# Decay tables in one 128-partition transfer, a plan that models instruction blocks, and the first tile's states in two parts

## The chip, the cores and the metric

The kernel runs on one core of one Trainium2 chip, one launch. The metric is device time in microseconds (us): 421.51, the median of three runs (421.35 to 424.3). Engines are named as in the profile: PE (matrix products; PEld its weight loads), DVE, ACT, POOL, and SP, whose queue issues all the DMAs.

## The reference, cut to what matters

Three layers in a row, on 4 sequences of 768 tokens with 256 channels:

```python
# 1: linear attention with decay, 8 heads, state 16 x 32 a head, in chunks
L = exp(cum[i] - cum[j]) * causal            # cum: running sum of log a
y = ((C @ B.T) * L) @ x + (C @ state) * exp(cum)
state = exp(cum[last]) * state + B.T @ (x * exp(cum[last] - cum))
# 2: channel mix; the row before each token is mixed in (mu_k, mu_r)
k = maximum(xk @ w_k, 0) ;  v = (k * k) @ w_v
x = sigmoid(xr @ w_r) * v
# 3: maxout
out = maximum(maximum(x @ w1, x @ w2), x @ w3) @ w_out
```

The weights come as 64-bit floats. Each product of layers 2 and 3 is made of three: both sides are split into a high and a low 32-bit part, and high x high, high x low and low x high are added.

## The kernel before, in words

The tokens are cut into 6 tiles of 4 x 128 = 512 columns. A tile t goes through `attention(t)` (layer 1, chunks of 64 tokens), `gate` (w_r), `ffn` (w_k in `s2(f)`, w_v in `s3(f)`, f = 0 to 7, L977 to L992), `combine`, `maxout(t)` (L1028, L1030) and `final` (w_out, L1068), and the tiles are interleaved: layer 3 of tile t - 1 runs beside layer 1 of tile t + 1.

The steps of `attention(t)` on PE: `spread` (the decay matrix of tiles 0 and 1: L680 for tile 0; L695 to L703 for tile 1, in two halves, into the banks pb), `gather` (L749: the state that each chunk adds), `cb` (L826: C times B), `carried` (L851: what the state before gives), `yt` (L861: the sums over values). Then `masked` (L756 on ACT, L758 on DVE) keeps the wanted blocks of what gather made, `state(c)` (L764, L766) decays the state by a column of the tile `ec` and adds, L815 makes `ce` from `ec`, and L896 copies y from PSUM into `xb`, from which `mix` (L928 to L931) makes the inputs of `gate` and `ffn`. From tile 2 on the decay matrix is not made by `spread`: it is loaded from a table in DRAM (L<-crd) and finished on DVE and ACT. `sums()` (L583, L594, L587, L588, L596) makes these tables and `ccol`; `ec` (decays to every token) is loaded from the table `ced`.

Weights: `load_split` loads one block (h, wd, wol and others are staging tiles), ACT takes the magnitude (L613), four DVE instructions build the 32-bit float (L614, L616, L618, L620), and L397 on ACT and L405 on DVE (or POOL) make the two parts. The staging tiles are reused: a block's DMA can be issued only when DVE has read the block before it out of its tile (L620).

The order of the work is not written out. Every step is an `op` with a cost for each engine it can run on, its buffers and a bias; the class `Plan` runs a list scheduler over them, 60 rounds, and issues the best order it has found. Each engine then executes its own list strictly in that order. The parts of the plan that the change touches:

- `BLOCK` and `CALM`: before, an op on PE marked as a burst (many small products) is put behind another one when more than 136 such products would fall into 4 us.
- `EARLY`: PE starts with 100 narrow products on zeros (L1131).
- `filler`: where the plan sees PE idle before the first `gate`, it issues products that nobody reads (L1129).
- `plan.wait_for`: the ops of which the earliest ends the stretch with fillers.

A program's instructions are themselves fetched by DMA, in blocks (the queues "instruction" in part 3 of the profile). The code in which the changed steps stand follows.

Of the kernel before, what the change touches and what calls it, by code (L numbers as in the profile page):

```python
# [75 lines left out]
class Plan:  # L76
# [16 lines left out]
    CALM = 4000.0  # L93
    BLOCK = 136
    HEAVY = (2100.0, 16000.0, 1300.0)
    WARM = (3400.0, 430.0, 215.0, 100.0, 600.0)
    EARLY = 100
# [39 lines left out]
    def forward(self, key, spare):  # L137
# [10 lines left out]
        runs = []  # L148
        done = 0

        def finish(i, e, now, fin):
            start[i], where[i], end[i] = now, e, fin
            for s in succ[i]:
                missing[s] -= 1
                ready_at[s] = max(ready_at[s], fin + self.lat(e, self.on[s]))
                if missing[s] == 0:
                    heapq.heappush(pending, (ready_at[s], s, ""))
                    heapq.heappush(events, ready_at[s])

        while done < n:  # L160
# [16 lines left out]
            for e in self.ENGINES:  # L177
# [5 lines left out]
                if e == "PE" and ops[q[0][1]][7] and ops[q[0][1]][7] + sum(  # L183
                        k for at, k in runs if at > now - self.CALM) > self.BLOCK:
# [34 lines left out]
                else:  # L219
                    if e == "PE" and now < self.COLD:  # L220
                        cost = cost * 1.35
                    if e == "PE" and ops[i][7]:
                        runs.append((now + cost, ops[i][7]))
# [104 lines left out]
def kernel(  # L328
# [242 lines left out]
    def initial():  # L571
        pe0 = boot.bufs[0]
# [170 lines left out]
    def gather(t, p):  # L743
        for b in range(NB):
            for q in range(NQ4):
                g = (q * NB + b) * 2
                for c in range(2):
# [21 lines left out]
    def attention(t):  # L769
# [11 lines left out]
        if first:  # L781
            inputs(0, FIRST)
        else:
            b_ec.writers, b_ec.readers = [dma(
                260, ec[32 * q:32 * q + 32].rearrange("p b c i -> p (b c i)"),
                ced[t * NG + q * NU:t * NG + (q + 1) * NU].rearrange("(r b) x -> r (b x)", r=2)[:, None, :].to_broadcast([NR, N, NU * HP]),
                r=[b_ced[t // (NT // 2)]], after=base, first=early) for q in range(NQ4)], []
# [12 lines left out]
        plan.bias += BIAS[5] * first  # L800
        if t < 2:
            op("PE", 64 * 10.8 + SWITCH, lambda: gather(t, U), r=[b_bd, b_xt[t]], w=U, burst=64)

        for c in range(2 if more else 1):
# [3 lines left out]
            else:  # L808
                masked(um[:, c], uv, [U[c]], [b_um[c]])
        if not first:  # L810
            state(0)
# [52 lines left out]
        if more:  # L864
            bias, plan.bias = plan.bias, 0.0
            inputs(t + 1, [EARLY1 * first] * 2)
# [16 lines left out]
        plan.bias -= BIAS[3] * first  # L883
        if more:
# [51 lines left out]
    def gate(half, t):  # L936
# [3 lines left out]
        for c2 in range(KC):  # L940
# [11 lines left out]
            plan.wait_for.append(begun['gate'])  # L952
# [5 lines left out]
    def ffn(half, t):  # L958
# [4 lines left out]
        def s2(f):  # L963
# [3 lines left out]
            def go():  # L967
                terms = []
                for c in range(KC):
                    terms.extend(three([w[:, c, fs] for w in wk_t], [v[:, cols] for v in xkt[c]]))  # L970
                mm3(p.ap[:, :n], terms)

            begun[f] = pe(6 * n * 0.4441, go, flat(b_xkt, hv) + [b_wk[c][f // 4] for c in range(KC)], [p])
# [211 lines left out]
```

## Time and profile before

| | |
|---|---|
| median of three runs | 421.51 us |
| profiled execution | 420.81 us |
| its span (first to last instruction) | 418.7 us |
| PE busy | 402.2 us, 96% |
| DVE busy | 260.4 us, 62% |
| ACT busy | 214.4 us, 51% |
| PE idle, by the table of waits | 12.9 us in 8 waits |

The span is cut into 40 slices in part 2 of the page; a digit is a tenth of the slice. PE stands at 9 in all but five slices (1, 3, 8, 23 and 39, counted from 0). DVE stands at 9 in many of the slices up to the fifteenth and falls to 4 or 5 afterwards. So the first third is shared by two engines near their limit, and after it PE alone is full.

### The profile page before, as it was taken

To read this page: it belongs to the slowest core of one execution; us is meant where nothing else is said; L and a number is where in the kernel's file an instruction comes from. 1 tells how busy PE (TensorE), PEld (TensorE's weight loads), DVE (VectorE), ACT (ScalarE), POOL (GpSimd) and SP (SyncE) were. 2 spreads that over 40 slices of the span, in tenths; PEclk is the share of its full clock that TensorE was granted. 3 is DMA by queue.
4 is the path that set the end of the run, shared out by engine and by line. 5 is a ranking of instruction groups with operands and counts; after the bars stand their busy time and mean duration, and the time that the engine had idled before them with its cause. 6 is when DMAs were issued, how large, how long until landed. Compare 5 with 4: busy or idle time off the path is not lost.

```text
span 418.7 us, 8689 instructions
## 1 busy us (share of the span) xinstructions
PE 402.2 (96%) x3681; PEld 320.1 (76%) x3681; DVE 260.4 (62%) x420; ACT 214.4 (51%) x374; POOL 54.2 (13%) x59
## 2 busy tenths in 40 slices
PE   9695999989999999999999989999999999999996
PEld 5464778768887888878888867888887888888885
DVE  5697889799997895465564466374465215440532
ACT  5575876786477672154762144763244752222221
POOL 4100000000200510142140033140022200010010
PEclk9789799999999999999999999999999999999999
DMA  7954636940126600022400000500000000001001
GB/s 251 392 160 138 201 88 204 266 125 2 53 92 178 159 26 0 17 89 77 125 25 2 10 19 2 125 2 26 0 3 2 25 25 2 0 0 44 8 2 50
DMA packets 12879, 31.55 MB, mean 75 GB/s; under 512 B 1768, under 2 KB 4136, under 8 KB 12072
## 3 DMA queue, kind: packets, MB, share of 16 engines
q1 hardware_dynamic: 12840, 30.99, 23.8%
q8 instruction: 29, 0.48, 0.5%
q14 instruction: 10, 0.08, 0.1%
HBM read 27.64 MB, written 3.34 MB: 74 GB/s over the span
## 4 chain that ended last, share of the span: by engine, by line
PE 73%; DVE 13%; DMA 7%; issue 3%; ACT 2%; SPq 1%; DVEq 0%; ACTq 0%
PE pa L665 40%; PE pa L992 13%; PE pa L1068 10%; PE pa L949 2%; DMA h<-in_w_v_dram 2%; DMA L<-crd 2%; PE pb L1068 2%; DVE tmp L1030 2%; DMA h<-in_w_r_dram 2%; PE pb L826 2%; DVE k2l L405 2%; SPq L410 1%; DMA ec<-ced 1%; PE pb L851 1%; PE pb L861 1%
## 5 line engine op out<-in xcount | busy, mean ns | idle before, releaser
L1030 DVE TENSOR_TENSOR tmp<-tmp,pa 128x512 f32<-128x512 f32 x72 | 48.9, 683 | 52.9 <-PE pa L665 52.1
L397 ACT ACTIVATE hr<-tmp 128x512 fp32r<-128x512 f32 x36 | 22.7, 632 | 75.2 <-DVE tmp L1030 74.8
L405 DVE TENSOR_TENSOR k2l<-tmp,k2h 128x512 fp32r<-128x512 f32 x52 | 37.3, 730 | 37.6 <-ACT tmp L980 30.8
L992 PE MATMUL pa<-k2l,wvh 128*128 128x512 f32 x96 | 38.0, 396 | 1.5 <-DVE k2l L405 1.5
L992 PE MATMUL pa<-k2h,wvh 128*128 128x512 f32 x96 | 38.1, 397 | 0.0
L992 PE MATMUL pa<-k2h,wvl 128*128 128x512 f32 x96 | 38.0, 396 | 0.0
L1068 PE MATMUL pa<-hr,worh 128*128 128x512 f32 x120 | 37.5, 393 | 0.0
L977 ACT ACTIVATE tmp<-pa 128x512 f32<-128x512 f32 x48 | 28.3, 591 | 10.9 <-PE pa L665 9.7
L978 ACT ACTIVATE k2h<-tmp 128x512 fp32r<-128x512 f32 x48 | 30.3, 631 | 3.0 <-PE pa L992 1.8
L1028 ACT ACTIVATE tmp<-pa 128x512 f32<-128x512 f32 x36 | 21.4, 594 | 18.3 <-PE pa L665 17.3
L405 DVE TENSOR_TENSOR hr<-tmp,hr 128x512 fp32r<-128x512 f32 x28 | 20.8, 745 | 13.4 <-ACT hr L397 13.3
L1068 PEld LDWEIGHTS pa<-hr,worh 128*128 128x128 f32 x120 | 22.2, 188 | 5.4 <-ACT th L954 0.6
L405 POOL TENSOR_TENSOR hr<-tmp,hr 128x512 fp32r<-128x512 f32 x8 | 10.8, 1354 | 108.0 <-ACT hr L397 108.0
L980 ACT ACTIVATE tmp<-tmp 128x512 f32<-128x512 f32 x37 | 23.2, 630 | 0.7
L1068 PE MATMUL pa<-hr,worl 128*128 128x512 f32 x60 | 23.3, 389 | 0.0
L992 PEld LDWEIGHTS pa<-k2l,wvh 128*128 128x128 f32 x96 | 18.0, 188 | 6.6 <-DVE k2l L405 2.6
L992 PEld LDWEIGHTS pa<-k2h,wvh 128*128 128x128 f32 x96 | 18.0, 188 | 4.3
L992 PEld LDWEIGHTS pa<-k2h,wvl 128*128 128x128 f32 x96 | 18.0, 188 | 4.2
L1039 ACT ACTIVATE outs<-pa 128x512 f32<-128x512 f32 x10 | 6.0, 597 | 23.9 <-PE pa L1068 23.9
L931 DVE SCALAR_TENSOR_TENSOR tmp<-xb,bits,tmp 128x512 f32<-128x512 f32 x24 | 17.4, 745 | 1.0 <-ACT tmp L929 0.8
L732 DVE TENSOR_TENSOR L<-L,future 128x512 f32<-128x512 f32 x16 | 11.4, 737 | 8.3 <-DMA L<-crd 8.3
L838 DVE TENSOR_TENSOR L<-pb,L 128x512 f32<-128x512 f32 (+1 forms) x28 | 15.7, 603 | 0.0
(271 smaller groups left out, 979.2 us busy)
## 6 DMA issues: line engine op xcount, KB each, us to landing
h<-in_w_dram SPq DMA_DIRECT2D x6, 768.0 KB
L<-crd SPq DMA_DIRECT2D x8, 512.0 KB
cw<-in_c_w_dram SPq DMA_DIRECT2D x6, 512.0 KB
xt<-in_x_l_dram SPq DMA_DIRECT2D x6, 512.0 KB
out_dram<-outs SPq DMA_DIRECT2D x10, 256.0 KB
h<-in_w_v_dram SPq DMA_DIRECT2D x2, 1024.0 KB
bt<-in_b_t_dram SPq DMA_DIRECT2D x6, 256.0 KB
bl<-in_b_l_dram SPq DMA_DIRECT2D x6, 256.0 KB
```

What stands on the lines that cost most here:

```text
L397: A.activation(ap(out_), ap(in_), AF.Copy)
L405: op({"DVE": tt(n), "POOL": pool(n, narrow)}, 0, lambda e: (V if e == "DVE" else G).tensor_sub(ap(out_), ap(x0), ap(x1)), r=r, w=w, after= ...
L665: T.matmul(pt, l, r_, start=(i == 0), stop=(i == last))
L838: op("DVE", tt(2 * step * HP), lambda q=q, b=b, lq=lq: V.tensor_mul(lq, W[q].ap[:, b * P:(b + step) * P].rearrange("p (b r i) -> p r b i", ...
L931: op("DVE", 61 + tt(n), lambda tv=tv, c=c: V.scalar_tensor_tensor(out=tv, in0=xb[:, c, bs, :P], scalar=om[:, i, c:c + 1], in1=tv, op0=ALU. ...
L977: op("ACT", 51 + 0.833 * n, lambda: A.activation(sq, p.ap[:, :n], AF.Relu), r=[p], w=[tm])
L978: op("ACT", act(n), lambda: A.activation(hi, sq, AF.Square), r=[tm], w=[kb])
L980: A.activation(sq, sq, AF.Square) if e == "ACT" else
L992: T.matmul(pv[c2].ap[:, :n], l, r_, start=(f == 0 and i == 0), stop=(f == FC - 1 and i == 2))
L1028: op("ACT", 51 + 0.833 * TW, lambda p=p, tm=tm: A.activation(tm.ap, p.ap, AF.Copy), r=[p], w=[tm])
L1030: op("DVE", tt(TW), lambda p=p, tm=tm: V.tensor_tensor(out=tm.ap, in0=tm.ap, in1=p.ap, op=ALU.max), r=[p], w=[tm])
L1068: T.matmul(p.ap, l, r_, start=(g == 0 and i == 0), stop=(g == GC - 1 and i == 2))
```

## The change

1. `ec` of tiles 1 to 5 comes in one transfer of 128 partitions in place of four of 32 (five DMAs for twenty). In the source, the four had an outer dimension of 2 (heads of a pair), repeated to 16 rows each; the one has an outer dimension of 8.
2. The plan counts PE's products and models blocks of 128 of them: a block can be entered only when it is loaded, and its load begins when the block before the last was left. The rule with `CALM` goes. `EARLY` is 140 in place of 100.
3. In tile 0, `gather` becomes two ops (chunk 0 early, chunk 1 after `yt` and `carried`), with the masks behind them; the inputs of tile 1 are declared later; `initial` uses bank pa 2 in place of 0.
4. `s2(0)` and `s2(1)` of tile 0 are each issued in two halves (by the two blocks of channels), and `wait_for` takes each half of `gate`.

```diff
@@ -90,11 +90,12 @@
     COLD = 7000.0
     FIRST = 1500.0
     STAY = 8000.0
-    CALM = 4000.0
-    BLOCK = 136
+    BLOCK, FRONT = 128, 92
+    FETCH = ((18000.0, 5600.0), (110000.0, 4200.0), (1e9, 2600.0))
+    OPEN = (1000.0, 28.0)
     HEAVY = (2100.0, 16000.0, 1300.0)
     WARM = (3400.0, 430.0, 215.0, 100.0, 600.0)
-    EARLY = 100
+    EARLY = 140
     ROUNDS = 60
     SPARE = (200.0, 1000.0)
     ENGINES = ("PE", "ACT", "POOL", "DVE", "SP")
@@ -145,7 +146,9 @@
         pending = [(0.0, i, None) for i in range(n) if not missing[i]]
         events = [0.0]
         dma = self.FIRST
-        runs = []
+        count, begun, edge = float(self.EARLY), 0.0, float(self.FRONT)
+        if count >= edge:
+            begun, edge = self.OPEN[0] + self.OPEN[1] * edge, edge + self.BLOCK
         done = 0
 
         def finish(i, e, now, fin):
@@ -156,6 +159,18 @@
                 if missing[s] == 0:
                     heapq.heappush(pending, (ready_at[s], s, ""))
                     heapq.heappush(events, ready_at[s])
+
+        def products(i):
+            return ops[i][7] or max(1, round(ops[i][0]["PE"] / 227.0))
+
+        def fetch(i, now):
+            cost, m, late, at, end = ops[i][0]["PE"], products(i), 0.0, begun, edge
+            while count + m >= end:
+                t = now + cost * (end - count) / m + late
+                free_at = at + next(k for lim, k in self.FETCH if at < lim)
+                late += max(0.0, free_at - t)
+                at, end = max(t, free_at), end + self.BLOCK
+            return late, at, end
 
         while done < n:
             now = heapq.heappop(events)
@@ -180,8 +195,7 @@
                     heapq.heappop(q)
                 if free[e] > now or not q:
                     continue
-                if e == "PE" and ops[q[0][1]][7] and ops[q[0][1]][7] + sum(
-                        k for at, k in runs if at > now - self.CALM) > self.BLOCK:
+                if e == "PE" and ops[q[0][1]][7] and fetch(q[0][1], now)[0] > 200.0:
                     like = min((k for k in q if not ops[k[1]][7] and where[k[1]] is None), default=None)
                     if like is not None and like[0] - q[0][0] < self.STAY:
                         q.remove(like)
@@ -219,8 +233,10 @@
                 else:
                     if e == "PE" and now < self.COLD:
                         cost = cost * 1.35
-                    if e == "PE" and ops[i][7]:
-                        runs.append((now + cost, ops[i][7]))
+                    if e == "PE":
+                        late, begun, edge = fetch(i, now)
+                        cost += late
+                        count += products(i)
                     free[e] = now + cost
                     fin = now + cost
                 heapq.heappush(events, free[e])
@@ -569,7 +585,7 @@
     plan.bias = 0.0
 
     def initial():
-        pe0 = boot.bufs[0]
+        pe0 = boot.bufs[2]
         lx = outr.bufs[1]
         lv = lx.ap[HP:].rearrange("p (b g n) -> p b g n", b=NB, n=N)
         copy(lv, la[HP:, :NG].rearrange("p (g b) -> p b g", b=NB)[:, :, :, None].to_broadcast([HP, NB, NQ4 * NR, N]), TW, [b_la], [lx])
@@ -740,11 +756,11 @@
         op({"DVE": tt(512), "POOL": pool(512)}, 0, lambda e: (V if e == "DVE" else G).tensor_mul(
             bd, bl, dfj[:, t * NG:(t + 1) * NG, None].to_broadcast([P, NG, N])), r=[b_bl, b_df], w=[b_bd], lock=True)
 
-    def gather(t, p):
+    def gather(t, p, blocks=(0, 1)):
         for b in range(NB):
             for q in range(NQ4):
                 g = (q * NB + b) * 2
-                for c in range(2):
+                for c in blocks:
                     cs = slice(c * HP, (c + 1) * HP)
                     T.matmul(p[c].ap[32 * q:32 * q + 32, TW // 2 + b * 2 * D:TW // 2 + (b + 1) * 2 * D], bd[cs, g:g + 2].rearrange("p r n -> p (r n)"),
                              xts[t % 2][cs, g:g + 2], start=True, stop=True, skip_group_check=True)
@@ -782,9 +798,9 @@
             inputs(0, FIRST)
         else:
             b_ec.writers, b_ec.readers = [dma(
-                260, ec[32 * q:32 * q + 32].rearrange("p b c i -> p (b c i)"),
-                ced[t * NG + q * NU:t * NG + (q + 1) * NU].rearrange("(r b) x -> r (b x)", r=2)[:, None, :].to_broadcast([NR, N, NU * HP]),
-                r=[b_ced[t // (NT // 2)]], after=base, first=early) for q in range(NQ4)], []
+                1100, ec.rearrange("p b c i -> p (b c i)"),
+                ced[t * NG:(t + 1) * NG].rearrange("(g b) x -> g (b x)", b=NB)[:, None, :].to_broadcast([NQ4 * NR, N, NU * HP]),
+                r=[b_ced[t // (NT // 2)]], after=base, first=early)], []
         if t < SPREAD:
             bias = plan.bias
             plan.bias = BIAS[2] if first else bias
@@ -798,15 +814,23 @@
         if first:
             initial()
         plan.bias += BIAS[5] * first
+
+        def states(k):
+            m = 32 * len(k)
+            op("PE", m * 10.8 + SWITCH * m / 64, lambda: gather(t, U, k), r=[b_bd, b_xt[t]], w=[U[c] for c in k], burst=m)
+
         if t < 2:
-            op("PE", 64 * 10.8 + SWITCH, lambda: gather(t, U), r=[b_bd, b_xt[t]], w=U, burst=64)
-
-        for c in range(2 if more else 1):
+            states((0,) if first else (0, 1))
+
+        def heads(c):
             uv = U[c].ap[:, TW // 2:].rearrange("p (b s d) -> p b s d", b=NB, s=2)
             if first and c == 0:
                 masked(sbd[:, 1], uv, [U[c]], [b_sbd[1]])
             else:
                 masked(um[:, c], uv, [U[c]], [b_um[c]])
+
+        for c in range(2 if more and not first else 1):
+            heads(c)
         if not first:
             state(0)
         c0 = 1 if first else 0
@@ -861,9 +885,9 @@
                             T.matmul(W[2 * (q // 2) + c].ap[k:k + 32, u * HP:(u + 1) * HP],
                                      xt[cs, (q * NB + u) * 2 + r], lt[cs, q, r, u],
                                      start=(first and u == 0), stop=not first, skip_group_check=True)
-        if more:
+        if more and not first:
             bias, plan.bias = plan.bias, 0.0
-            inputs(t + 1, [EARLY1 * first] * 2)
+            inputs(t + 1)
             plan.bias = bias
         ahead = more and not first
 
@@ -881,6 +905,12 @@
         if not first:
             sums_of_values()
         plan.bias -= BIAS[3] * first
+        if first:
+            states((1,))
+            heads(1)
+            bias, plan.bias = plan.bias, 0.0
+            inputs(1, [EARLY1] * 2)
+            plan.bias = bias
         if more:
             state(1)
         if not first:
@@ -949,7 +979,7 @@
                             T.matmul(p.ap[:, :n], l, r_, start=(c == 0 and i == 0), stop=(c == KC - 1 and i == 2))
 
                 begun['gate'] = pe(3 * len(ks) * n * 0.4441, go, flat([b_xr[c] for c in ks], hv) + [b_wr], [p])
-            plan.wait_for.append(begun['gate'])
+                plan.wait_for.append(begun['gate'])
             tb = thr.next()
             op("ACT", 51 + 0.833 * n, lambda p=p, tb=tb: A.activation(
                 tb.ap[:, :n], p.ap[:, :n], AF.Tanh, scale=0.5), r=[p], w=[tb])
@@ -964,13 +994,14 @@
             p = pm.next()
             fs = slice(f * P, (f + 1) * P)
 
-            def go():
-                terms = []
-                for c in range(KC):
-                    terms.extend(three([w[:, c, fs] for w in wk_t], [v[:, cols] for v in xkt[c]]))
-                mm3(p.ap[:, :n], terms)
-
-            begun[f] = pe(6 * n * 0.4441, go, flat(b_xkt, hv) + [b_wk[c][f // 4] for c in range(KC)], [p])
+            for ks in ((0,), (1,)) if t == 0 and f < 2 else ((0, 1),):
+
+                def go(ks=ks):
+                    for c in ks:
+                        for i, (l, r_) in enumerate(three([w[:, c, fs] for w in wk_t], [v[:, cols] for v in xkt[c]])):
+                            T.matmul(p.ap[:, :n], l, r_, start=(c == 0 and i == 0), stop=(c == KC - 1 and i == 2))
+
+                begun[f] = pe(3 * len(ks) * n * 0.4441, go, flat([b_xkt[c] for c in ks], hv) + [b_wk[c][f // 4] for c in ks], [p])
             tm, kb = tmp.next(), k2r.next()
             k2[f] = kb
             sq, hi, lo = tm.ap[:, :n], kb.ap[0][:, :n], kb.ap[1][:, :n]
```

The plan makes a new order out of this. Three places of it, for PE, ACT and DVE; lines are those of each kernel (L749 is L765 in the changed one, L826 L850, L851 L875, L861 L885, L613 L629, L977 L1008, L756 L772, L764 L780, L1030 L1061).

PE in tile 0, from the second half of `yt` on, first before. A row merges equal instructions; a 32-bit product is two in the profile's count.

```order
L576 MATMUL pa_131<-ccol,outs_114 128x64 x4
L861 MATMUL pb_135<-L,xt_121 32x64 x8
L861 MATMUL pb_136<-L,xt_121 32x64 x8
L861 MATMUL pb_135<-L,xt_121 32x64 x8
L861 MATMUL pb_136<-L,xt_121 32x64 x8
L749 MATMUL pa_131<-xt_121,bd 32x64
L749 MATMUL pa_132<-xt_121,bd 32x64
L749 MATMUL pa_131<-xt_121,bd 32x64
```

```order
L765 MATMUL pa_131<-xt_121,bd 32x64 x16
L885 MATMUL pb_135<-L,xt_121 32x64 x8
L885 MATMUL pb_136<-L,xt_121 32x64 x8
L885 MATMUL pb_135<-L,xt_121 32x64 x8
L885 MATMUL pb_136<-L,xt_121 32x64 x8
L592 MATMUL pa_133<-ccol,outs_114 128x64 x4
L885 MATMUL pb_135<-L,xt_121 32x64 x8
L885 MATMUL pb_136<-L,xt_121 32x64 x8
L885 MATMUL pb_135<-L,xt_121 32x64 x8
L885 MATMUL pb_136<-L,xt_121 32x64 x8
L875 MATMUL pb_135<-ce,sbd 64x64 x2
```

The 16 products of gather's first half now stand ahead of all of `yt`; before, all 32 followed it. Ahead of these rows stand 40 more narrow products.

ACT, the first evacuations of `s2` (pa0_131 and pa1_132 are its two banks, wd_98<-h2_93 is the second block of w_v), before and now.

```order
L711 ACTIVATE L_120<-pb1_136 128x8x64 x2
L613 ACTIVATE wd_98<-h2_93 128x1024
L977 ACTIVATE tmp0_107<-pa0_131 128x512
L756 ACTIVATE um_126<-pb0_135,bits_128 128x4x32 x2
L978 ACTIVATE k2h0_99<-tmp0_107 128x512
L977 ACTIVATE tmp1_108<-pa1_132 128x512
L980 ACTIVATE tmp0_107<-tmp0_107 128x512
L978 ACTIVATE k2h1_101<-tmp1_108 128x512
```

```order
L727 ACTIVATE L_120<-pb1_136 128x8x64 x2
L1008 ACTIVATE tmp0_107<-pa0_131 128x512
L1009 ACTIVATE k2h0_99<-tmp0_107 128x512
L629 ACTIVATE wd_98<-h2_93 128x1024
L1008 ACTIVATE tmp1_108<-pa1_132 128x512
L772 ACTIVATE um_126<-pb0_135,bits_128 128x4x32 x2
L1008 ACTIVATE tmp2_109<-pa0_131 128x512
L772 ACTIVATE um_126<-pb0_135,bits_128 128x4x32 x2
```

The evacuation of the first bank and its square (L1008, L1009) now stand ahead of the second block of w_v; the evacuation of the second bank stands behind it, as before.

DVE in tile 3 (the same in tile 4): the two decays of the state, with the maxout steps between them, before and now.

```order
L764 TENSOR_TENSOR sbd_127<-sbd_127,ec_119 128x256
L740 TENSOR_TENSOR bd_125<-bl_124,dfj_123 128x512
L1030 TENSOR_TENSOR tmp3_110<-tmp3_110,pa2_133 128x512
L1030 TENSOR_TENSOR tmp2_109<-tmp2_109,pa0_131 128x512
L764 TENSOR_TENSOR sbd_127<-sbd_127,ec_119 128x256
L1030 TENSOR_TENSOR tmp3_110<-tmp3_110,pa3_134 128x512
L405 TENSOR_TENSOR hr2_1445<-tmp2_109,hr2_1445 128x512
```

```order
L780 TENSOR_TENSOR sbd_127<-sbd_127,ec_119 128x256
L756 TENSOR_TENSOR bd_125<-bl_124,dfj_123 128x512
L1061 TENSOR_TENSOR tmp3_110<-tmp3_110,pa2_133 128x512
L780 TENSOR_TENSOR sbd_127<-sbd_127,ec_119 128x256
L1061 TENSOR_TENSOR tmp2_109<-tmp2_109,pa0_131 128x512
L1061 TENSOR_TENSOR tmp3_110<-tmp3_110,pa3_134 128x512
L421 TENSOR_TENSOR hr2_1543<-tmp3_110,hr2_1543 128x512
```

The second decay (the one of `state(0)` of the next tile, which reads the new `ec`) stands one place earlier: two maxout steps follow it where one did.

On SP's queue the first block of w_v now stands ahead of the tables' stores (it stood behind them and behind the first `ec`), and the one `ec` ahead of the second block of w_v.

## Rows read from the trace of the kernel before

**Rows 1.** Head of the page: span, busy time (share) and instructions.

```profile
span 418.7 us, 8689 instructions
...
PE 402.2 (96%) x3681; PEld 320.1 (76%) x3681; DVE 260.4 (62%) x420; ACT 214.4 (51%) x374; POOL 54.2 (13%) x59
```

**Rows 2.** Who waited for whom: total us, times, longest; PE.

```profile
PE pa L665 <- ACT tmp L1028: 2.6, 2, 1.6
```

**Rows 3.** Timeline (start, duration, [idle before]), PE, first 33 us.

```profile
11.22 0.86 PE L861 MATMUL pb<-L,xt 64*32 64x64 f32 x64
...
17.28 0.67 PE L749 MATMUL pa<-xt,bd 64*32 64x64 f32 x30 [2.70 <-issue]
18.76 1.13 PE L851 MATMUL pb<-ce,sbd 32*64 32x64 f32 x32 [0.81 <-ACT sbd L756]
...
24.80 0.38 PE L695 MATMUL pb<-future,identb 128*128 128x512 bf16 x1
...
32.69 0.50 PE L665 MATMUL pa<-xk00h,wkh 128*128 128x512 f32 x1
```

**Rows 4.** DMA queues: packets, MB, share of 16 engines; whole span.

```profile
q8 instruction: 29, 0.48, 0.5%
```

**Rows 5.** Timeline, ACT, 23 to 41 us.

```profile
23.36 1.14 ACT L397 ACTIVATE k2h<-tmp 128x512 fp32r<-128x512 f32 x2
24.40 0.32 ACT L596 ACTIVATE ccol<-pb 128x192 f32<-128x192 f32 x1
...
39.54 1.12 ACT L613 ACTIVATE wd<-h 128x1024 f32<-128x1024 f32 x1 [4.74 <-DMA h<-in_w_v_dram]
40.55 0.59 ACT L977 ACTIVATE tmp<-pa 128x512 f32<-128x512 f32 x1
```

**Rows 6.** Timeline, SP's queue: when DMAs were issued.

```profile
0.81 0.38 SPq L410 DMA_DIRECT2D la<-in_a_l_dram  x1
...
26.61 2.15 SPq L410 DMA_DIRECT2D ec<-ced  x3
30.08 0.35 SPq L410 DMA_DIRECT2D h<-in_w_v_dram  x1
...
173.04 2.64 SPq L410 DMA_DIRECT2D ec<-ced  x4
```

**Rows 7.** Timeline, PE, 41 to 70 us.

```profile
41.20 0.80 PE L665 MATMUL pa<-xk00h,wkh 128*128 128x512 f32 x1 [4.31 <-ACT tmp L977]
...
44.06 2.01 PE L826 MATMUL pb<-cw,bt 32*64 32x128 f32 x64
...
68.54 1.21 PE L826 MATMUL pb<-cw,bt 32*64 32x128 f32 x64
```

**Rows 8.** Stretches: length, busy PE PEld DVE ACT POOL, PEclk, DMA share, GB/s.

```profile
17.30:20.00 2.70, 1.89 (x63) 1.48 (x63) 1.37 (x4) 1.72 (x4) 0.00 (x0) 0.50 1.06 412
18.00:126.80 108.80, 102.23 (x1224) 78.82 (x1224) 100.18 (x165) 75.93 (x135) 2.80 (x1) 0.95 0.46 140
42.00:44.00 2.00, 2.00 (x5) 1.11 (x4) 1.90 (x4) 1.70 (x4) 0.00 (x0) 0.50 0.36 31
48.00:52.00 4.00, 4.00 (x19) 3.28 (x18) 3.61 (x7) 3.69 (x6) 0.00 (x0) 1.00 0.80 251
178.00:180.60 2.60, 2.60 (x134) 2.02 (x134) 0.02 (x1) 0.63 (x1) 0.00 (x0) 1.00 0.12 45
```

**Rows 9.** Timeline, DVE.

```profile
2.88 0.28 DVE L549 TENSOR_SCALAR la<-la 128x224 f32<-128x224 f32 x1 [1.90 <-DMA la<-in_a_l_dram]
...
18.13 0.42 DVE L758 TENSOR_TENSOR um<-pa,bits 128x256 f32<-128x256 f32 x1 [2.12 <-PE pa L749]
...
176.04 0.69 DVE L1030 TENSOR_TENSOR tmp<-tmp,pa 128x512 f32<-128x512 f32 x1 [2.43 <-PE pa L665]
...
180.79 0.42 DVE L764 TENSOR_TENSOR sbd<-sbd,ec 128x256 f32<-128x256 f32 x1 [2.77 <-DMA ec<-ced]
...
245.48 0.42 DVE L764 TENSOR_TENSOR sbd<-sbd,ec 128x256 f32<-128x256 f32 x1 [3.36 <-DMA ec<-ced]
```

## The prediction, made blind

> **What bounds the kernel now.** I read the head of the page first: PE is busy for 96% of the span, DVE for 62% [rows 1]. So whatever this change gives must come out of the few us in which PE idles or works slowly; its products stay the same but for the narrow ones and the fillers, 13 before and 4 in the new order. The stretches show DVE near its limit in the first third: busy for 100.18 of the 108.80 us from 18 to 126.8 [rows 8]. The table of waits and PE's timeline then name three places. **(A)** PE stops for 2.70 us in the middle of tile 0's gather, waiting for nothing the profile shows, then 0.81 us for ACT's mask [rows 3]; DVE idles 2.12 us for the same gather [rows 9]. **(B)** PE stops for 4.31 us behind L977, the evacuation of a bank [rows 7]; ACT reaches it only after the second block of w_v, for which it stood 4.74 us [rows 5]. PE is slow afterwards. **(C)** PE waits twice, 2.6 us in all, for L1028 [rows 2]; just before both, DVE stands at L764 for `ec`, 2.77 and 3.36 us [rows 9], with a maxout step and the copy of y queued behind.
>
> My sums are against the profiled execution: span 418.7, its own time 420.81. The median of the runs, 421.51, lies 0.7 above.
>
> **A: the stop, and the front of tile 0.** PE's 3,681 products and as many weight loads [rows 1] over 29 packets [rows 4] are some 127 products a packet, so I take the stop for a block that was not there. Counted in the program, it falls at the 349th product. One block earlier, the 222nd, lies 40 products into the `yt` of 11.22 [rows 3], at about 11.8: the block took 17.28 - 11.8 = 5.5 us. In the new order 40 more narrow products and gather's first half stand ahead of `yt`, and the 222nd is in that half. Half of what 40 narrow products cost (1.1 us, as 100 take 2.8) is taken up by waits for DVE there, so that half runs at about 11.7 and the block is there at 17.2, as before. The stop does not go: it moves into the second half of `yt`, where some 40 of 64 products are left. Behind it stand these (0.9, as 30 take 0.67) and `carried` (1.13), but no mask, which now works earlier: `carried` ends at 19.3 where it ended at 19.89, 0.6 earlier. Then tile 1's spread waits for `ccol`, L596 on ACT, which ends at 24.72 (PE goes on at 24.80) [rows 3, 5]. The new order takes two casts (1.14) and one scaling from ahead of it and puts a mask of about the scaling's length there: 1.2 earlier. **A gives 1.8** (0.5 to 2.5). DVE's 2.12 us go too: the new order puts w_r's and w_k's steps there.
>
> **B: w_v.** Before, w_v's second block was issued at 30.08, behind four `ec`, three of them from 26.61 [rows 6], and ACT got it at 39.54. Now the first block goes out at about 18.6 (behind w_k's L620, which is earlier on DVE) and is in before the second is issued at about 28. With one `ec` on the queue it should be in by 33. ACT has L977's successor ahead of it and needs it only after `s2(0)`, at some 33. So the 4.31 us go. So does the slow stretch behind them: the granted clock there is 0.50, the lower level of 1.2 GHz, after PE's idling [rows 8]. Five products in 2.0 us against 19 in 4.0 [rows 8] are 0.19 more for each of six, 1.1; `cb` takes 2.01 in place of 1.21 [rows 7], 0.8; the next products, not yet back at 2.4 GHz, about 0.8. **B gives 7.0** (3 to 7). Halving `s2(0)` and `s2(1)` costs nothing: the same products, each waiting for its own channels.
>
> **What DVE gives back.** A and B bring PE 8.8 forward, DVE must follow. It idled 108.80 - 100.18 = 8.6 us up to 126.8 [rows 8], and 2.1 before 18.13 [rows 9]; it gets one product of w_r from POOL, 0.6. It could come 10.1 forward with no idling at all. I leave it a third of the 10.7, since it must still stand before `combine` of tile 0 for the last w_v product, and its staging waits for loads: 10.1 - 3.6 = 6.5. **Back go 2.3** (0 to 6).
>
> **C: `ec`.** While nothing but `ec` is on the queue, the share of 16 DMA engines is 0.12, two engines, at 45 GB/s [rows 8]. From the first issue at 173.04 [rows 6] to DVE's going on at 180.79 it is 7.7 us [rows 9]. The new second L764 stands one place earlier, behind the L1030 that ends at 176.73 [rows 9]: the transfer costs nothing if it lands within 3.7 us. The nearest row of a single 128-partition transfer is `la`, issued at 0.81, used at 2.88: 2.1 us [rows 6, 9], though of less than half the bytes. The bounds are 2.1 and 7.7; I take a value below 3.7, the nearer row's side. SP gains 2 us a tile, which hides. **C gives 2.6** (0 to 2.6): both waits for L1028.
>
> The Trainium skill says why two (DMA: Bandwidth & Descriptors, "Why a DMA increments its semaphore by 16 and not by 1"): a transfer runs on the largest number of engines up to 16 that divides the outer dimension of both sides. The trace agrees for the two. By that rule the new one gets 8, not 16; an estimate, 1.5 us plus a quarter of 6.2, is 3.0: the sum stays, the margin shrinks from 1.6 to 0.7.
>
> **The sum:** -1.8 - 7.0 + 2.3 - 2.6 = -9.1, so 411.7 for the profiled execution, **412.4** on the median's scale.
>
> **The rivals.**
> 1. *DVE holds the front.* DVE keeps 6.6 of its 10.7 us of idling, since each load of weights waits for DVE to free the staging tile; PE then stops for halves of k squared (L405). The front gives 10.1 - 6.6 = 3.5: 415.4. For it: 100.18 of 108.80 busy. Against: the waits went with A and B. 0.16.
> 2. *`ec` lands no sooner*, so the change does not do there what it says. C gives 0: 415.0. Against it is the share of 0.12, which a wider transfer should raise. 0.06.
> 3. *w_v's second block is still late.* PE then waits some 2.5 us before `s2(3)` and slows again (2.7): the front gives 3.6: 415.3. For it: queue share 1.06 at 17.3 to 20 [rows 8], when the first block would start. 0.07.
> 4. *PE stays slow in the front.* Nine fillers fewer are issued, and PE idles behind the moved stop; the granted clock from 17.3 to 20 was 0.50 [rows 8]. If spread and `gate` of tile 0 ran at 1.2 GHz, 12 products of `gate` cost 2.3 more and spread, scaled like `cb`, 1.9: A and B give 4.6: 414.3. 0.06. The Trainium skill (TensorE: Matmul & The Clock Gate, Part 1) has it that the lower clock is the default and activity lifts it; by that rule taking fillers out speaks against the change.
> 5. *Slower.* The one `ec` is drained by one engine in place of two: twice 6.2 plus 1.5 is 13.9, 6.2 later than now. DVE stands in front of three maxout steps in tiles 2, 3 and 4, and PE behind it: 3 x 6.2 = 18.6 against the front's 6.5: 433.6. It decides from a landing some 2.2 us later than now. For it: I see no transfer of this form in the trace. 0.05.
>
> **How the numbers follow.** My forecast has 0.60. 1% is about what a measurement of this kernel can tell from no change: 417.3 and 425.7. All cases but the fifth lie below 417.3, the first four with some of their spread above; I put faster at 0.86, within 1% at 0.09, slower at 0.05. Low end: A 2.5, B 7, no giving back, C 2.6 and the small waits behind L405: 408.8. High end: the front gives 2.5 and C 1: 418.0. Outside are the fifth case and the edges.
>
> **What would show it.** A: a wait for nothing shown of about 3 us inside L885, `carried` ending near 19.3, spread at 23.5. B: no wait of PE above 1 us between 33 and 45, the granted clock at 1.00 there, w_v's second block landed before 33. DVE: idle below 4 us from 18 to 118, the first maxout steps 6 to 7 us earlier. C: no DVE wait on `ec`, no PE wait for L1059, an `ec` landing about 3 us after its issue. I am wrong if PE's new waits between 40 and 80 sum to more than 4 us, if `ec` still lands 7 us after its issue, or if another stop for nothing shown appears.

## The result, and the profile after

The changed kernel takes 409.93 us (median of 4 runs, 409.4 to 410.64) against 421.43 for the one before, run on the same chip (421.02 to 424.3). The ratio is 0.971, with a 95% interval of 0.967 to 0.976. The profiled execution took 410.0 us: 10.8 less than the one that the sum was made against. The forecast was 412.4, in a range of 408.8 to 418.0.

The head of the page after, to be read against [rows 1]:

```profile
span 408.1 us, 8724 instructions
PE 399.6 (98%) x3712; PEld 320.0 (78%) x3712; DVE 257.6 (63%) x424; ACT 214.6 (53%) x377; POOL 49.3 (12%) x55
```

PE's waits after (line waited at, what ended it: us in total, times, longest; `issue` stands where the profile shows nothing that was waited for):

```profile
PE pb L885 <- issue: 2.3, 1, 2.3
PE pa L1162 <- DVE xb L559: 1.0, 1, 1.0
PE pb L599 <- DVE xb L926: 0.7, 1, 0.7
PE pa L1002 <- ACT tmp L1008: 0.5, 2, 0.3
```

The 4.3 us behind the evacuation (L977 before, L1008 now) are 0.5, and the two waits for the maxout copy [rows 2] (L1028, now L1059) have no row any more. The stop for nothing shown is still there.

PE's timeline of the front (start, duration, line; what it waited for in brackets). It answers to [rows 3]; narrow products, the first product on data, `cb`, gather, `yt`, `carried`, the first product of `sums()`, spread, `s2(0)`:

```profile
1.01 3.90 PE L1162 MATMUL pa<-sbd 128*32 128x16 bf16 x140 [1.01 <-DVE xb L559]
5.24 0.85 PE L582 MATMUL pb<-la,ccol 128*128 128x192 f32 x2
12.26 0.69 PE L850 MATMUL pb<-cw,bt 32*64 32x128 f32 x32
12.89 0.65 PE L765 MATMUL pa<-xt,bd 64*32 64x64 f32 x32
15.58 0.43 PE L885 MATMUL pb<-L,xt 64*32 64x64 f32 x27
18.34 0.75 PE L885 MATMUL pb<-L,xt 64*32 64x64 f32 x37 [2.33 <-issue]
19.02 1.13 PE L875 MATMUL pb<-ce,sbd 32*64 32x64 f32 x32
...
21.88 1.17 PE L599 MATMUL pb<-tri,la 128*96 128x128 f32 x4 [0.72 <-DVE xb L926]
...
24.76 0.63 PE L711 MATMUL pb<-future,identb 128*128 128x512 bf16 x1
33.01 0.50 PE L1002 MATMUL pa<-xk00h,wkh 128*128 128x512 f32 x1
```

The stop has moved into the second half of `yt`, as forecast, but it ends at 18.34. `carried` ends at 20.15 (19.89 before), spread starts at 24.76 (24.80) and `s2(0)` at 33.01 (32.69): the front has gained nothing up to here.

SP's issues, ACT's steps about w_v's second block (the wd load), and the second use of `ec` on DVE, against [rows 5], [rows 6] and [rows 9]:

```profile
20.69 0.33 SPq L426 DMA_DIRECT2D h<-in_w_v_dram  x1
28.27 0.74 SPq L426 DMA_DIRECT2D ec<-ced  x1
30.15 0.36 SPq L426 DMA_DIRECT2D h<-in_w_v_dram  x1
...
35.45 0.60 ACT L1008 ACTIVATE tmp<-pa 128x512 f32<-128x512 f32 x1 [1.18 <-PE pa L1002]
36.92 1.13 ACT L629 ACTIVATE wd<-h 128x1024 f32<-128x1024 f32 x1 [0.21 <-DMA h<-in_w_v_dram]
...
165.53 0.62 SPq L426 DMA_DIRECT2D ec<-ced  x1
...
169.14 0.42 DVE L780 TENSOR_TENSOR sbd<-sbd,ec 128x256 f32<-128x256 f32 x1
```

w_v's second block was issued at 30.15, 30.08 before, but ACT had it 6.8 us later in place of 9.5. `ec` costs DVE no wait.

Four stretches of the windows (length, busy us of PE, PEld, DVE, ACT and POOL, granted clock, share of the 16 DMA engines, GB/s), against [rows 8]:

```profile
18.00:118.00 100.00, 98.24 (x1279) 76.67 (x1279) 98.83 (x164) 74.89 (x137) 0.00 (x0) 0.97 0.50 153
25.00:26.00 1.00, 1.00 (x5) 0.64 (x4) 0.85 (x3) 1.00 (x3) 0.00 (x0) 0.76 1.01 412
33.00:45.00 12.00, 11.82 (x176) 8.97 (x169) 11.46 (x15) 10.58 (x22) 0.00 (x0) 1.00 0.53 166
167.50:168.00 0.50, 0.50 (x4) 0.42 (x3) 0.00 (x0) 0.26 (x1) 0.00 (x0) 1.00 0.51 201
```

DVE, the third engine column, idles 1.2 us between 18 and 118; before it was 8.6, up to 118 as up to 126.8. From 33 to 45 PE has the full clock. The last row is `ec` alone on the queue: half of the 16 engines, 201 GB/s, where the four transfers had an eighth and 45 GB/s [rows 8].

### The profile page after: what moved, and what is told of

Read it like the earlier page. It is cut to its first block, busy times and chain, and to the rows that moved or that the text cites. A ratio compares the mean times of both kernels' runs of the same rounds, so it can differ in the third digit from the quotient of the medians.

```text
span 408.1 us, 8724 instructions
## 1 busy us (share of the span) xinstructions
PE 399.6 (98%) x3712; PEld 320.0 (78%) x3712; DVE 257.6 (63%) x424; ACT 214.6 (53%) x377; POOL 49.3 (12%) x55
## 4 chain that ended last, share of the span: by engine, by line
PE 81%; DVE 12%; DMA 2%; ACT 2%; issue 2%; DVEq 0%; SPq 0%; ACTq 0%
PE pa L681 30%; PE pa L1002 14%; PE pa L1023 14%; PE pa L1099 10%; PE pa L979 3%; PE pb L1099 2%; DMA h<-in_w_v_dram 2%; DVE tmp L1061 2%; PE pb L850 1%; DVE k2l L421 1%; PE pb L885 1%; PE pb L875 1%; PE pa L1162 1%; PE pa L696 1%; DVE tmp L961 1%
## 5 line engine op out<-in xcount | busy, mean ns | idle before, releaser
L1061 DVE TENSOR_TENSOR tmp<-tmp,pa 128x512 f32<-128x512 f32 x72 | 49.1, 685 | 56.4 <-PE pa L681 55.4
L1008 ACT ACTIVATE tmp<-pa 128x512 f32<-128x512 f32 x48 | 28.4, 594 | 11.6 <-PE pa L1002 8.3
L1059 ACT ACTIVATE tmp<-pa 128x512 f32<-128x512 f32 x36 | 21.5, 597 | 20.8 <-PE pa L681 18.4
L1009 ACT ACTIVATE k2h<-tmp 128x512 fp32r<-128x512 f32 x48 | 30.2, 633 | 2.6 <-PE pa L1023 1.2
L421 DVE TENSOR_TENSOR hr<-tmp,hr 128x512 fp32r<-128x512 f32 x28 | 19.2, 690 | 14.8 <-ACT hr L413 14.7
L782 POOL TENSOR_TENSOR sbd<-sbd,um 128x256 f32<-128x256 f32 x2 | 4.2, 2107 | 147.9 <-DVE sbd L780 147.9
```

What stands on the lines that cost most here:

```text
L421: op({"DVE": tt(n), "POOL": pool(n, narrow)}, 0, lambda e: (V if e == "DVE" else G).tensor_sub(ap(out_), ap(x0), ap(x1)), r=r, w=w, after= ...
L1008: op("ACT", 51 + 0.833 * n, lambda: A.activation(sq, p.ap[:, :n], AF.Relu), r=[p], w=[tm])
L1009: op("ACT", act(n), lambda: A.activation(hi, sq, AF.Square), r=[tm], w=[kb])
L1059: op("ACT", 51 + 0.833 * TW, lambda p=p, tm=tm: A.activation(tm.ap, p.ap, AF.Copy), r=[p], w=[tm])
L1061: op("DVE", tt(TW), lambda p=p, tm=tm: V.tensor_tensor(out=tm.ap, in0=tm.ap, in1=p.ap, op=ALU.max), r=[p], w=[tm])
```

## The experiments

"Changed" is the kernel after the change. Where an order is called kept, the lists of all engines are those of that kernel but for the named edit. Every run is timed in turns with the kernel before on its chip; the ratio is to that (its medians there were 420.8 to 422.2, so between chips a difference of medians is good to about 1 us).

| run | us | ratio, 95% interval |
|---|---|---|
| changed | 409.93 | 0.971 (0.967 to 0.976) |
| ec_four | 418.33 | 0.994 (0.991 to 0.997) |
| ec_four_after_wv | 415.01 | 0.984 (0.982 to 0.986) |
| ec_two | 410.27 | 0.974 (0.971 to 0.976) |
| ec_one_in_before | 412.14 | 0.979 (0.976 to 0.983) |
| act_swap_in_before | 420.50 | 1.000 (0.997 to 1.002) |
| before_ec_one_replanned | 413.89 | 0.981 (0.979 to 0.983) |
| old_planner | 414.20 | 0.982 (0.978 to 0.986) |
| no_split | 411.12 | 0.975 (0.972 to 0.977) |
| dve_work_added | 418.46 | 0.991 (0.989 to 0.993) |
| narrow_100 | 409.91 | 0.974 (0.970 to 0.978) |
| narrow_180 | 412.24 | 0.977 (0.975 to 0.979) |
| narrow_120_replanned | 409.53 | 0.971 (0.968 to 0.974) |

### The transfer, undone in the changed kernel and done alone in the one before

ec_four: the changed kernel, order kept.

```diff
-    1100, ec.rearrange("p b c i -> p (b c i)"),
-    ced[t * NG:(t + 1) * NG].rearrange("(g b) x -> g (b x)", b=NB)[:, None, :].to_broadcast([NQ4 * NR, N, NU * HP]),
+    lambda: [Q.dma_start(ec[32 * q:32 * q + 32].rearrange("p b c i -> p (b c i)"),
+    ced[t * NG + q * NU:t * NG + (q + 1) * NU].rearrange("(r b) x -> r (b x)", r=2)[:, None, :].to_broadcast([NR, N, NU * HP])) for q in range(NQ4)]
```

> The changed kernel with its own order, but each ec again as four transfers of 32 partitions, issued one behind the other. My theory: ec lands 7.7 us after its issue in place of 3.0, DVE stands for it twice for 3 to 4 us (tiles 3 and 4, the second L780), PE waits 2.6 to 3.5 us behind it; and SP reaches the second w_v block 1 to 2 us later, which ACT needs almost at once (it waits 0.21 us now), another 1 us: 412.5 to 414.5. Rival 1: the 1.9 us that came after 118 us are the new order's and not the transfer's: 410, with DVE standing elsewhere. Rival 2: the front hangs on ec too (w_v and the decays of tile 2 behind it on SP): 416 or more.

418.33 us: 8.4 of the gain are lost, about twice what I expected, so the second rival (the front hangs on `ec`) is right as well. SP, ACT and PE in the front, and DVE at the `ec` of tile 4:

```profile
31.05 0.36 SPq L426 DMA_DIRECT2D h<-in_w_v_dram  x1
...
38.95 1.12 ACT L629 ACTIVATE wd<-h 128x1024 f32<-128x1024 f32 x1 [2.70 <-DMA h<-in_w_v_dram]
40.60 0.50 PE L1002 MATMUL pa<-xk00h,wkh 128*128 128x512 f32 x1 [2.65 <-ACT tmp L1008]
177.10 0.43 DVE L780 TENSOR_TENSOR sbd<-sbd,ec 128x256 f32<-128x256 f32 x1 [3.48 <-DMA ec<-ced]
```

Its windows show why w_v is late (clock, DMA share and GB/s are the last three columns):

```profile
30.00:31.00 1.00, 1.00 (x6) 0.68 (x6) 1.00 (x3) 0.77 (x2) 0.00 (x0) 1.00 0.13 49
38.00:39.00 1.00, 0.00 (x0) 0.00 (x0) 0.00 (x0) 0.05 (x1) 0.00 (x0) 1.00 0.13 49
42.00:44.00 2.00, 2.00 (x7) 1.51 (x6) 2.00 (x4) 2.00 (x5) 0.00 (x0) 0.50 0.51 57
```

At 30 to 31 `ec` moves on two engines (0.13 of 16). At 38 to 39, when `ec` should be long done, the share is 0.13 again: ACT is still waiting for w_v's block, so that is its rest, at the rate of two engines. That they are the two that `ec` was on is inferred. And after PE's wait its clock is at 0.50, the lower level, for several products.

ec_one_in_before: the same edit the other way round, in the kernel before, its order kept (the one transfer at the place of the first of the four).

> The kernel before with its own order, but ec as one transfer of 128 partitions at the place of the first of the four. My theory: the two waits for L1028 go (2.6), and w_v's second block is issued some 2 us sooner, so PE's 4.31 us shrink to 2.3: 416.8 to 418.8. Rival: the transfer alone does nothing here, since DVE is late with other things: 421.

412.14 us, 8.7 less, again about twice my larger figure. The issue of w_v's second block, ACT's step on it and PE behind that; ACT and PE stood 4.74 and 4.31 us before [rows 5, 7]:

```profile
30.82 0.35 SPq L410 DMA_DIRECT2D h<-in_w_v_dram  x1
...
36.40 1.16 ACT L613 ACTIVATE wd<-h 128x1024 f32<-128x1024 f32 x1 [0.98 <-DMA h<-in_w_v_dram]
38.10 0.50 PE L665 MATMUL pa<-xk00h,wkh 128*128 128x512 f32 x1 [0.48 <-ACT tmp L977]
```

ACT still takes that step ahead of the evacuation here. So the wait in B goes without any new order. Nor is it SP's time for the issues: the block was issued 0.7 us later than before (30.82, 30.08 before), but ACT had it 5.6 us after that in place of 9.5.

### ACT's part of the order, alone

act_swap_in_before: the kernel before, one ACT instruction moved.

```diff
     plan.arrange()
+    plan.start[plan.late] = plan.start[plan.behind] + 5.0   # wd L613 of w_v's 2nd block; L977 of s2(1)
```

> The kernel before with one ACT instruction moved: the first step on w_v's second block stands behind the evacuations of the first two blocks of k, everything else in its place. PE's wait of 4.31 us and the slow stretch behind it then go, all but a wait of 1 to 2 us two blocks on; at the sixth block PE is some 5.4 us earlier. Theory PE: that is what the kernel gains, less a third: 417.5 to 416. Theory DVE: what counts is DVE's idling up to 118 us; its 2.56 us behind the same w_v block stay, 0.7 and 0.4 go at once and the 2.45 for L go only if PE lets SP issue it sooner: gain 1 to 4, 417.5 to 420.5, with new PE waits for DVE between 45 and 80 us.

420.50 us: no change. Theory PE is refuted; theory DVE names the right loss, and of its gain only the low end, 1 us, is still inside the interval. PE and DVE of this run (L666, L978 and L994 are L665, L977 and L992 of before):

```profile
46.50 0.50 PE L666 MATMUL pa<-xk00h,wkh 128*128 128x512 f32 x1 [1.82 <-ACT tmp L978]
82.56 0.51 PE L994 MATMUL pa<-k2l,wvh 128*128 128x512 f32 x1 [1.94 <-DVE k2l L405]
...
41.49 0.69 DVE L614 TENSOR_SCALAR wd<-wd 128x1024 f32<-128x1024 f32 x1 [2.06 <-ACT wd L613]
81.22 0.69 DVE L733 TENSOR_TENSOR L<-L,future 128x512 f32<-128x512 f32 x1 [5.11 <-DMA L<-crd]
```

PE's 4.31 us are gone but for 1.82 two blocks on, and its slow stretch with them. But DVE still waits for w_v's block (2.06 us, 2.56 before), and then 5.11 us for the decays of tile 2 (2.45 before), which PE pays 1.94 for. What PE won ahead of DVE was given back where DVE met the next late transfer.

### Which part of ec's cost is w_v's

ec_four_after_wv: ec_four with tile 1's `ec` behind w_v's second block on SP.

```diff
     plan.arrange()
+    plan.start[plan.late] = plan.start[plan.ahead] + 5.0   # SP: ec of tile 1 behind w_v's 2nd block
```

> As the run with four transfers for ec in the changed kernel (418.3), but tile 1's four are issued behind w_v's second block on SP in place of ahead of it; nothing else moved. Theory of the queue: what cost the front was that w_v's second block stood behind ec on the two engines that carry ec; now it is issued at about 30.1 and in by 37, ACT's wait for it (2.70 us) falls under 0.5 and PE's 2.65 goes, with the slow products behind it: 3.5 to 4 us back, 414.3 to 415. What is left against 409.9 is ec landing late in tiles 3 and 4. Rival: w_v lands late for another reason (four issues on SP, or the decays and loads about it): no change, 418.

415.01 us, as expected; the rival's 418 is out. SP, ACT and DVE (L781 is L780):

```profile
29.71 0.35 SPq L426 DMA_DIRECT2D h<-in_w_v_dram  x1
30.16 2.71 SPq L801 DMA_DIRECT2D ec<-ced  x4
...
35.96 1.12 ACT L629 ACTIVATE wd<-h 128x1024 f32<-128x1024 f32 x1
...
172.82 0.42 DVE L781 TENSOR_TENSOR sbd<-sbd,ec 128x256 f32<-128x256 f32 x1 [3.80 <-DMA ec<-ced]
```

ACT waits no more. So 3.3 us of the change (418.33 to 415.01; 4.3 by the ratios) are w_v's block being late behind `ec`. The run moves two things at once: with the four `ec` ahead, SP issued the block 1.3 us later (31.05 against 29.71), and it then took 7.9 us to reach ACT in place of at most 6.3. How the 3.3 us are shared between the two it doesn't tell; in ec_one_in_before the second alone did the work. The other 5.1 (415.01 to 409.93; 5.2 by the ratios) are `ec` landing late for tiles 3 to 5.

ec_two: the changed kernel, order kept, two transfers of 64 partitions.

```diff
+    lambda: [Q.dma_start(ec[64 * q:64 * q + 64].rearrange("p b c i -> p (b c i)"),
+    ced[t * NG + 2 * q * NU:t * NG + 2 * (q + 1) * NU].rearrange("(r b) x -> r (b x)", r=4)[:, None, :].to_broadcast([4, N, NU * HP])) for q in range(2)]
```

> The changed kernel with its own order, ec in two transfers of 64 partitions. If a transfer runs on as many engines as its source's outer dimension allows (2 groups of 16 partitions before: two engines; 8 now: eight), each of these runs on four: a share of 0.25 while nothing else is on the queue, landing 4 to 5 us after the issue. DVE then waits 1 us or less at the second L780 of tiles 3 and 4, and w_v's second block is some 1 us late: 410.5 to 412.5. Rival: only one single transfer helps, the count of engines is not the cause: share 0.12, 416 to 418.

410.27 us, a little better than forecast, and the share is a quarter (window, then DVE):

```profile
168.50:169.00 0.50, 0.50 (x4) 0.41 (x3) 0.34 (x1) 0.00 (x0) 0.00 (x0) 1.00 0.26 102
...
170.16 0.42 DVE L780 TENSOR_TENSOR sbd<-sbd,ec 128x256 f32<-128x256 f32 x1 [1.31 <-DMA ec<-ced]
```

Outer dimensions of 2, 4 and 8 gave 0.13, 0.26 and 0.51 of 16 engines, at 49, 102 and 201 GB/s. The rival (only a single transfer helps) is out. DVE's 1.3 us no longer reach PE, and the time can't be told from that with eight engines. The Trainium skill's rule on the count of engines (DMA: Bandwidth & Descriptors, "Why a DMA increments its semaphore by 16 and not by 1") agrees with all three. It also says that on such a queue these are the lowest-numbered ones; that w_v's rest moved at 0.13 after `ec` agrees, though no row here names the engines.

### DVE, and the rest of the change

dve_work_added: the changed kernel, order kept, one DVE step of eight weight blocks done twice (the result stays the same).

```diff
-op("DVE", tt(m), lambda: V.scalar_tensor_tensor(out=lu, in0=low, scalar=29, ...))
+op("DVE", tt(m), lambda: [V.scalar_tensor_tensor(out=lu, in0=low, scalar=29, ...) for _ in range(2 if m > TW and not place else 1)])
```

> The changed kernel with its own order; the last DVE step on each of w_v's, w1's, w2's and w3's eight blocks is done twice (it changes nothing the second time): 2 x 1.14 and 6 x 0.87 = 7.5 us more on DVE, all between 38 and 101 us. Theory: DVE bounds the stretch from 18 to 118 us (98.8 of 100.0 us busy), so it costs nearly all of it: 7.5 less the 1.2 it idles, 416 to 417.5. Rival: PE bounds it and DVE has slack behind its queue: 3 us or less, 410 to 413.

418.46 us: 7.5 us of DVE work cost 8.5 (8.3 by the ratios), all of it. DVE bounds this stretch of the changed kernel. Its busy time in the windows, 105.5 of 108:

```profile
18.00:126.00 108.00, 100.89 (x1276) 76.24 (x1263) 105.50 (x168) 75.27 (x136) 0.00 (x0) 0.96 0.45 143
```

before_ec_one_replanned: the kernel before with the single transfer, as in the change's part 1, planned anew.

> The kernel before with the single ec transfer as in the change, and the planner left free to order the work about it (with the old rule on blocks and no split of the gather). With the order of before kept, the one transfer gave 412.1. Theory: the rest of the change (2.2 us) is the planner's freedom with a shorter ec, which also lets ACT evacuate before w_v's second block: 410 to 411. Rival: it is the gather in two parts and the planner's blocks: 412 to 413.

413.89 us: neither my theory nor, quite, the rival. The planner's freedom gains nothing over the kept order (412.14; the intervals overlap), and a second stop appears.

```profile
58.94 0.66 PE L861 MATMUL pb<-L,xt 64*32 64x64 f32 x42 [2.88 <-issue]
```

old_planner: the changed kernel with the class `Plan` of before (`EARLY` 140), planned anew.

> The changed kernel with the planner's rule on instruction blocks as it was before, 140 narrow products, everything else as in the change, and the order planned anew. Theory: the block rule pays by keeping runs of small products apart; without it a second stop of PE for nothing shown turns up where such runs stand close, near 50 to 60 us, as the 2.88 us at 58.9 in the kernel before with one ec planned anew: 412 to 414. Rival: the split gather and the one ec are the whole gain, the rule nothing: 409.5 to 410.5.

414.20 us, 4.3 more than the changed kernel, with a second stop at the place forecast, but a smaller one. The larger part is ACT's again:

```profile
58.46 1.08 PE L869 MATMUL pb<-L,xt 64*32 64x64 f32 x86 [1.18 <-issue]
71.67 0.50 PE L986 MATMUL pa<-xk10h,wkh 128*128 128x512 f32 x1 [2.24 <-ACT tmp L992]
```

The order of the new rule is worth some 4 us against an order made anew without it; how much of that is the stop avoided and how much a lucky order, the run doesn't tell.

no_split: the changed kernel with part 3 undone, planned anew.

> The changed kernel with the first tile's states in one part again, the order planned anew (new block rule, 140 narrow products, one ec). Theory: the split gives 1 to 2.5 us: the mask of the first half and the scaling no longer stand behind the stop, ACT has them 4 us sooner. Without it 411 to 412.5. Rival: the stop is the same 5.5 us block whatever stands there: 409.5 to 410.5.

411.12 us. The interval overlaps that of the changed kernel (0.972 to 0.977 against 0.967 to 0.976), so the 1.2 us are not established.

### The stop in the front

narrow_100 and narrow_180: the changed kernel, order kept, other counts of narrow products.

```diff
-for _ in range(0 if idle else self.EARLY):
+for _ in range(0 if idle else 100):    # 180 in the other run
```

> The changed kernel with its own order, but 100 narrow products ahead of the first product in place of 140. Theory of blocks: the stop is where the program passes a count of some 350 products, and ends 5.5 us after the 222nd; it moves 40 products on, to the first products of carried (L875), still ends at 18.2 to 18.4, and carried ends at 19.4 in place of 20.15: 409.2 to 409.9. Rival: the stop belongs to the place in the program (its data or its bank); it stays 27 products into the second half of yt and ends 1.1 earlier, at 17.3: 409.0. Rival 2: fewer products, lower clock for longer: slower, 410.5 or more.

> The changed kernel with its own order, 180 narrow products in place of 140. Theory of blocks: the 222nd product falls into the second cb (L850 of the first half) at 10.5 to 11, the stop moves 40 products back, into the first half of yt, and ends at 16 to 16.6 instead of 18.3; the rest of the front is 1.1 us later for the 40 products, so carried ends about 19, 1 us earlier; a next stop then ends near 22, in the second part of the gather. 409 to 410.5. Rival: the stop's end is set by the load on the queue and not by the 222nd product: it ends at 18 to 19.4 as in the other runs, 410.5 to 411.5.

PE of the first run, then of the second:

```profile
17.34 0.32 PE L875 MATMUL pb<-ce,sbd 32*64 32x64 f32 x3 [1.10 <-DVE ce L839]
19.46 0.96 PE L875 MATMUL pb<-ce,sbd 32*64 32x64 f32 x29 [1.80 <-issue]
```

```profile
15.57 0.81 PE L885 MATMUL pb<-L,xt 64*32 64x64 f32 x59 [0.22 <-DVE L L862]
17.23 0.31 PE L885 MATMUL pb<-L,xt 64*32 64x64 f32 x5 [0.85 <-issue]
24.62 1.17 PE L599 MATMUL pb<-tri,la 128*96 128x128 f32 x4 [2.21 <-DVE xb L926]
```

The stop moves by 40 products each way, to the fourth product of `carried` and into the first half of `yt`: the theory of blocks holds and the place in the program is not the cause. But I had its end wrong by a us: in the first run the 222nd product came at 13.7, since PE waited for DVE (1.07 us) ahead of `yt`; in the second at 11.8. The next stop that I expected near 22 did not come: 128 products further on, at 21.8, only some 4.5 us after the end of the first stop, PE went through without one. So 5.5 us is the time of this block and not of every one. The time didn't move with 100 (409.91). With 180 it is 2.3 us longer (412.24), but the intervals still touch (0.975 to 0.979 against 0.967 to 0.976), so that isn't established; there the later steps came later, and `carried` ended at 21.4.

narrow_120_replanned: the changed kernel with `EARLY = 120`, planned anew.

> The changed kernel planned anew with 120 narrow products in place of 140; the planner's own model has it 0.4 us shorter. Theory: the stop follows the 222nd product, which is in the gather either way, so it ends within 0.5 of 18 us; DVE bounds the stretch behind it: 409 to 410.3, no measurable change. Rival: the half of the narrow products that is saved comes through: 408.5 to 409.

409.53 us, the same as the changed kernel within the intervals. I found no version that is clearly faster.

## Why the prediction was right, and where it was not

The time fell into the range, but the terms were not what I took them for.

**A (1.8) failed.** The step that failed reads "Half of what 40 narrow products cost (1.1 us, as 100 take 2.8) is taken up by waits for DVE there, so that half runs at about 11.7". Up to gather nothing took it up: the first product on data started at 5.24 in place of 4.17, and the second `cb` at 12.26 in place of 10.60 (narrow_100 has it at 10.58), so gather's first half ran at 12.89. The wait for DVE stands only behind it, ahead of `yt` (0.22 us; 1.07 in narrow_100). The rest of the step was right: the 222nd product came at 12.9, the stop ended 5.4 us later (5.5 forecast), inside the second `yt`. The other part of A, 1.2 us at `ccol`, failed elsewhere: ACT had the casts out of the way, but the product that feeds it (L599, L583 before) started at 21.88 in place of 21.08, behind gather's second half and 0.72 us of waiting for DVE's copy of `xb`. A gave nothing.

**B (7.0) came about, by another cause.** PE's waits and slow products there are gone but for 0.2 us, the clock was 1.00 from 33 to 45, and the first w_v block was issued at 20.69, 2 us after the forecast. But I put the gain mainly down to the order: w_v's first block out of the way, and ACT's evacuation ahead of the second. ACT's part of the order alone gave nothing in the kernel before, the whole new order with four transfers left PE a wait of 2.65 us there (ec_four), and the transfer alone took the wait away in the kernel before. I counted the four `ec` as issues on SP and hadn't asked which engines they hold up. The trace of before would have said so: w_v's second block took 9.5 us to ACT [rows 5, 6], and in its last two, the share of the DMA engines was that of two engines:

```profile
37.00:38.00 1.00, 0.00 (x0) 0.00 (x0) 1.00 (x1) 0.00 (x0) 0.00 (x0) 1.00 0.16 61
38.00:39.00 1.00, 0.00 (x0) 0.00 (x0) 0.13 (x1) 0.00 (x0) 0.00 (x0) 1.00 0.12 51
```

After the change it landed at 36.9, not before 33; ACT took the evacuation first and waited 0.21 us.

**DVE's give-back (2.3) did not come.** DVE's idling fell from 8.6 us to 1.2, so it gave back next to nothing; I had left it a third. Rival 1 was right that DVE bounds the stretch (7.5 us of work added cost 8.5), wrong that its waits for loads stay: with the transfer alone in the kernel before, it no longer waits above 0.2 us behind a weight block, and is busy for 96.4 of the 100 us.

**C (2.6) was mis-sized.** The mechanism held: `ec` of tile 4 lands 3.0 us after its issue, DVE and PE don't wait. With the four transfers in the changed kernel it costs 5.1 us, as DVE then stands for `ec` in three tiles (1.88, 3.80 and 4.09 us in ec_four_after_wv), and PE waits for DVE behind the last two, 3.4 us in all. After the second of these its clock fell to 0.50:

```profile
240.00:242.00 2.00, 2.00 (x6) 1.56 (x5) 1.80 (x2) 0.66 (x2) 1.01 (x1) 0.50 0.00 0
```

The forecast's 3.0 us for eight engines rests on a split of 7.7 us into 1.5 and 6.2 for which no row of before stands. The landings come near it: 7.7 us after the first issue on two engines, 5.0 on four (ec_two; 4.6 by the split), 3.0 on eight.

So of the 10.9 us that these runs add up to, 8.4 are the transfer's (3.3 by w_v, 5.1 by its own landing; 8.7 when done alone), and some 2.5 the new order, the split and the narrow products together (ec_four against before, 0.994; the halves of `s2` were not run alone). I had them the other way about: 2.6 for the transfer's own landing, and 6.5 for the front, mostly the order's. Two errors cancelled; that the total fits is luck. Rivals 2, 3 and 5 didn't occur; the fifth is excluded by the share of 0.51. The fourth showed in its first part only: the clock was still 0.76 from 25 to 26, where it had been 1.00 from 24 on before, and the first half of spread took some 0.4 us longer; `gate` had 1.00.

## What to carry to other kernels

Read the DMA share while one transfer is alone on the queue: an eighth means two engines, and then ask not only who waits for this transfer but which later one is spread over all engines and will stand behind it on those two. A wait of PE that goes away by reordering gains nothing while another engine still meets late transfers (DVE here, for 2.06 and 5.11 us in act_swap_in_before). And when a forecast comes out right, undo its parts one by one before believing its terms.

## What the runs showed of the hardware

- A transfer's tail can stand behind an earlier transfer on few engines: w_v's 1 MB block reached ACT 9.5, 9.0 and 7.9 us after its issue with `ec` on two engines ahead of it (before, act_swap_in_before, ec_four), 6.9 with `ec` on four, 6.8 and 5.6 on eight (changed, ec_one_in_before).
- PE's instructions come in blocks of some 128 products with their loads. In all fourteen profiles PE stopped in front of the 350th or 351st product, whatever stood there, until 5.3 to 6.0 us after the 222nd or 223rd. The Trainium skill (Runtime: NRT & Kernel Launch, "Instruction fetch mechanics") gives 256 instructions a block, which agrees, and calls the cost of a block's edge mostly hidden; with products this small, and a DMA share of 1.02 from 9 to 18 us, it was 0.85 to 3.1 us here, and the measurement decides.
- Runs of small products at 55 to 59 us met such a stop again in three orders (1.18, 1.31 and 2.88 us), in front of the 988th or 989th product, some five times 128 behind the first stop.
